# All scores of a segment in one part of the down stage of a retention and SwiGLU kernel

## The chip, the cores and the metric

The kernel runs on one core of a Trainium2 chip. The metric is the device time of one execution in microseconds (us), as the median of several runs. A profiled execution is a run of its own with the hardware profiler on; its time differs a little from that of the runs without it.

Five engines work side by side, each on its own list of instructions in a fixed order: TensorE (PE; its weight loads are shown as PEld), VectorE (DVE), ScalarE (ACT), GpSimd (POOL) and SyncE (SP). SP issues nearly all transfers (DMA) between the chip's memory (DRAM) and the on-chip memory (SBUF). PE writes its results into eight accumulator banks of 128 rows by 512 floats. An engine waits for another by semaphores, and an instruction that waits holds up all that stand behind it on its engine.

## The reference

The kernel computes a retention over 4 batches, 8 heads, 768 positions and 64 dimensions per head, and passes its output through a SwiGLU block:

```python
gamma = 1.0 - 2.0 ** (-5.0 - np.arange(H))          # H = 8
state = zeros(B, H, D, D)                            # B = 4, D = 64
for t in range(S):                                   # S = 768
    state = gamma * state + k[:, :, t]^T v[:, :, t]  # per batch and head
    y[:, :, t] = 1/sqrt(D) * q[:, :, t] @ state
x = y.transpose(0, 2, 1, 3).reshape(B * S, H * D)    # 3072 x 512
g = x @ w_gate                                       # 512 x 1536
out = (g * sigmoid(g) * (x @ w_val)) @ w_out         # 1536 x 512
```

In the kernel the retention is done in chunks of 128 positions. Inside a chunk the scores k q are multiplied by a mask of decays and then applied to v; what came before a chunk enters through a 64x64 state per head, which is decayed and added to from chunk to chunk.

## The kernel before

**Segments and stages.** The 3072 tokens are worked on in four segments, 0 to 3, of 768 tokens each. A segment is three chunk positions of two batches. Each segment has an up stage (the products with w_gate and w_val, 12 tiles f of 128 rows of the hidden dimension) and a down stage (the product with w_out). In segment 0 the up stage uses plain products (lines 896 and 914), and the weights are converted and written back on the way; the up stages of segments 1 to 3 use seven products per tile, called p{f}.0 to p{f}.6 (`up3`, line 1065), each of six 128x384 matmuls. The steps that process these products are called u{f}.0 to u{f}.9; they work in banks 0 and 1, 2+f%2 and 6+f%2.

Numbers are kept in float32 and split into three parts for the matmuls. Helpers record these splits, so many operations share a line: 968 (ACT), 971 (DVE), 974 (POOL or DVE) for weights and hidden values, 977 (ACT), 980 (POOL), 984 (DVE) for the rest. Items live in a ring of slots, and a load into a slot waits until the last reader of the slot is done.

**Down stage.** It consists of 72 steps D{f}.{tok} (`down`, line 1128): for each f in 0 to 11 and each 128-token block tok in 0 to 5, three 128x512 matmuls accumulate into bank tok. A step needs h{f} (the three splits h{f}.0 to .2 of the hidden tile on ACT, DVE and DVE) and the weight item W{f}. In segment 0, W{f} is a load of the plain weights, which d{f}.0 (ACT), d{f}.1 (POOL) and d{f}.2 (DVE) split, and Z{f} writes the result back to DRAM; in later segments W{f} loads the split weights (768 KB). At the end e{tok} brings each bank out.

**Retention within the down stage.** While the down stage of segment s runs, the retention of segment s+1 is computed in steps between the D steps. The chunk positions of the segment are three pairs p = 0, 1, 2, each with a chunk of two batches. For each pair:

- l{n} (`load_pair`, line 752; n = 4p+w with w = 0, 1, 2, 3 for k, q, v and k in its other layout) loads operands to the place that HOME gives; each l{n} moves two tiles of 128x512 floats on SP.
- sc{p} (`scores_of`, line 776): 64 matmuls of 64x64 into two banks.
- dec{p}.0 and .1 (`decayed`, line 786): DVE multiplies each bank with the mask and stores 128x512 into SBUF.
- q{p}.0 and .1 (`scale_q2`, DVE and POOL), k{p}.0 and .1 (`scale_k2`, ACT, in one case POOL) scale q and k.
- A{p}, B{p}, C{p} (`mix_a`, `mix_b`, `mix_c`): matmuls of 64x64 into banks 6 and 7; they give the outputs y and what is added to the state.
- was{p}.z (`decay2`, ACT) decays the state, new{p}.z (`keep_state`) adds to it.
- y{p}.zj (`bring_y`, line 999): 16 copies on ACT per pair out of banks 6 and 7; sum{p}.m and x{p}.n.k make the operands of the next up stage from them.

sc0 uses banks 4 and 5, sc1 and sc2 use banks 6 and 7. The decayed scores of p = 0 and 2 lie in `tmp`, those of p = 1 in `tab` (called `spare`). Since D steps use banks 0 to 5, a D step on bank 4 or 5 that starts the accumulation must wait for dec0, and A, B, C of one pair and sc of the next share banks 6 and 7.

**Order.** The order of all steps is written out by hand: PLAN is a list of 2371 step names, which `run` (line 452) plays, and each step's instructions go to their engines in that order. A name begins with the segment: "0/D0.3" is a step of segment 0's down stage and "1/A0" a step of segment 1's retention. The constants PARTS, COST, LOADS and UNITS and the times given with each step say which steps exist, and matter for the order only where PLAN does not name a step. On PE the three down stages with retention begin like this:

```
segment 0: 1/sc0 D0.0 D0.2 D0.1 D0.4 D0.5 D0.3 1/A0 D1.0 D1.4 1/B0
segment 1: p11.4 2/sc0 p11.6 D0.2 D0.3 D0.4 D0.1 D1.1 D0.5 D0.0 D1.4 D1.5 D1.0 2/A0
segment 2: D0.2 3/sc0 p11.6 D0.1 D0.0 D0.3 D0.4 D1.2 D1.1 D0.5 D1.3 D1.4 D1.5 D1.0 D2.3 3/A0
```

The functions that the diff touches:

Of the kernel before, what the change touches and what calls it, by code (L numbers as in the profile page):

```python
# [18 lines left out]
B, H, S, D = 4, 8, 768, 64  # L19
# [6 lines left out]
L = 3  # L26
# [24 lines left out]
    l0:0 l1:0 A0 A1 s0 U0:0 l0:2 l0:3 a0:1 s1 b0:1 A2 h0 S0:1 m0 K0 x0:2 c0:1 l2:0 x0:1 l2:1  # L51
    l1:3 C0:1 t0 l1:2 V0:0 l3:1 n0:0 s2 a0:0 Q2 l3:0 l2:3 n0:1 b0:0 S0:0 m1 k1 x1:1 x1:2 l2:2
    c0:0 n0:2 U1:1 C0:0 t1 o2 l3:3 g2 s3 n0:3 n0:4 l4:1 p0:0 m2 a1:1 x2:1 k2 q3 b1:1 l4:0 a1:0
    x2:2 S1:1 l5:1 l3:2 n0:5 c1:1 k3 t2 C1:1 o3 b1:0 l5:0 l4:2 g3 v0:0 s4 S1:0 t3 l5:2 c1:0 C1:0
    U2:0 m3 s5 U12:3 U3:1 q5 q4 u0:0 a2 o5 o4 T0:0 n1:0 m4 b2 y0:0 x3:1 x3:2 m5 T0:1 n1:1 n1:3
    T0:2 S2 n1:2 p0:1 v0:1 n1:4 T1:0 x4:1 u0:1 y0:1 a12 n1:5 x5:1 U4:0 T1:1 a3 p1:0 x4:2 u1:0
    p1:1 x5:2 Z0 u1:1 T1:2 c12 v1:0 U5:1 y1:0 v1:1 p0:2 Z1 l5:3 v0:2 c2 C2 b12 y1:1 p1:2 n2:0 a4
    U6:0 u0:2 b3 n2:1 u1:2 v1:2 S12 n2:3 L y0:2 S3 c3 n2:2 U13:2 G2:0 i2:0 n2:4 y1:2 C3 g4 T2:0
    b4 T2:1 n3:0 C12 n2:5 G2:1 i2:1 a5 T2:2 n3:1 Z2 n3:2 S4 n3:3 n3:4 c4 T3:0 C4 W2:0 j2:0 T3:1
    W2:1 G3:1 U7:1 c13 T3:2 G3:0 n4:0 Z12 n3:5 n4:1 i3:1 W3:0 Z3 n4:2 b5 a6 j2:1 i3:0 S5 n4:3  # L60
    G4:1 n4:4 c5 W3:1 T4:0 h2 U8:0 C5 T4:1 T4:2 n4:5 G4:0 a13 i4:1 n5:0 j3:0 n5:1 n5:3 n5:2 b6
    U14:3 i4:0 a7 W4:0 n5:4 j3:1 G5:1 S6 c6 b13 Z4 j4:0 T5:0 T5:1 C6 W4:1 n6:0 U9:1 T5:2 n5:5 b7
    a8 S13 W5:0 G5:0 j4:1 c14 Z5 W5:1 i5:0 i5:1 n6:1 S7 j5:1 n6:3 n6:4 c7 a9 C7 n7:0 n6:2 G6:0
    U10:0 j5:0 b8 G6:1 T6:0 n7:1 n7:3 S8 C13 T6:1 i6:1 i6:0 n6:5 n7:2 c8 Z13 l4:3 a14 n7:4 b14
    W6:1 W6:0 T6:2 C8 T7:0 S14 U15:2 n7:5 n8:0 j6:0 G7:1 j6:1 i7:1 U11:1 C14 b9 G7:0 n8:3 W7:1
    S9 n8:1 c15 n8:2 W7:0 c9 Z6 i7:0 j7:1 a10 P1 C9 n8:4 G8:1 n8:5 T7:1 j7:0 n9:0 b10 Z14 k4
    U16:3 g5 T7:2 S10 T8:0 G8:0 n9:1 a15 b15 P2 c10 Z7 W8:0 T8:1 n9:2 S15 T8:2 Z8 W8:1 C15 C10
    n9:3 i8:1 i8:0 k5 G9:1 Z15 a11 b11 j8:0 j8:1 n10:0 n9:4 S11 n9:5 t4 U17:2 c16 n10:1 G9:0
    T9:0 i9:0 t5 n10:3 n10:2 W9:1 a16 b16 n10:4 n10:5 S16 W9:0 T9:1 j9:0 P0 i9:1 c11 0/h0.0
    G10:0 G10:1 C11 n11:0 j9:1 W10:1 n11:3 i10:0 C16 Z16 i10:1 T9:2 n11:4 Z9 T11:0 T11:1 n11:5  # L70
    a17 b17 T11:2 W10:0 n11:1 T10:0 Z11 0/h0.1 S17 T10:1 j10:0 0/W0 c17 0/h1.0 n11:2 h1 G11:0
    C17 j10:1 i11:0 0/d0.0 G11:1 1/sc0 1/dec0.0 0/W1 1/l3 1/l5 1/q0.0 i11:1 0/h2.0 0/d0.1 0/h0.2
    0/h4.0 0/d1.0 W11:0 0/d0.2 1/k0.0 W11:1 1/l4 j11:0 0/D0.0 0/D0.2 1/dec0.1 0/d1.1 j11:1
    0/h1.1 0/D0.1 0/d1.2 0/W2 1/q0.1 0/D0.4 1/k0.1 1/was0.0 0/D0.5 0/Z0 0/h1.2 0/h2.1 0/D0.3
    T10:2 0/d2.0 Z17 0/h3.0 1/A0 1/new0.0 0/D1.0 0/h3.1 0/Z1 0/d2.1 0/D1.4 1/B0 1/y0.01 0/h4.1
    0/W3 1/y0.05 Z10 1/y0.06 1/y0.03 1/y0.00 1/y0.02 1/y0.04 0/D1.3 0/d2.2 1/begin 1/y0.07
    0/D1.1 1/was0.1 0/h2.2 0/d3.0 0/D1.5 0/h4.2 0/D1.2 1/C0 1/y0.12 1/y0.15 1/y0.11 1/y0.14 0/Z2
    0/d3.1 1/y0.10 0/h3.2 1/y0.17 1/y0.16 0/D2.3 1/y0.13 1/x0.2.0 0/D2.2 1/new0.1 0/d3.2 0/D2.4
    0/W4 1/sum0.0 0/D2.1 1/sum0.1 1/x0.2.1 0/D2.0 0/D2.5 1/x0.1.0 1/l7 0/Z3 0/h5.0 1/sum0.3
    1/x0.1.1 0/d4.0 0/d4.1 1/x0.1.2 1/sc1 1/dec1.1 0/D3.2 1/q1.1 1/sum0.2 1/l6 1/dec1.0 0/D3.4  # L80
    1/q1.0 0/D3.1 0/W5 0/D3.3 0/d4.2 0/h5.1 1/was1.0 1/k1.1 0/D3.5 0/D4.4 1/k1.0 0/D3.0 0/D4.3
    0/h6.0 1/A1 1/l8 0/d5.0 1/x0.2.2 0/D4.2 1/l9 0/D4.5 0/W6 0/d5.1 0/h5.2 0/h6.1 1/x0.0.0
    0/D4.0 0/D4.1 1/new1.0 0/h7.0 0/d6.0 1/B1 1/x0.0.1 0/d5.2 1/y1.01 0/D5.1 0/D5.2 0/Z4 1/y1.06
    1/y1.02 1/y1.00 0/h8.0 0/D5.4 1/y1.05 0/D5.3 0/D5.0 1/y1.07 1/y1.04 0/h6.2 0/W7 1/y1.03
    0/d6.1 1/was1.1 1/x0.0.2 1/C1 0/d7.0 0/h7.1 0/h7.2 1/y1.17 0/Z5 0/d6.2 1/l11 0/D6.2 0/D6.0
    0/D5.5 1/y1.10 1/y1.15 0/h8.1 1/y1.11 1/y1.16 0/d7.1 1/y1.14 1/y1.12 1/y1.13 1/x1.2.0 0/Z6
# [1217 lines left out]
```

## Time and profile before

| what | value |
|---|---|
| median of 3 runs | 648.2 us (647.91 to 648.77) |
| profiled execution | 652.34 us, span 650.5 us, mean granted clock of PE 0.995 |
| PE busy | 635.7 us (98%) |
| PEld busy | 581.5 us (89%) |
| DVE busy | 489.6 us (75%) |
| ACT busy | 392.4 us (60%) |
| POOL busy | 272.3 us (42%) |
| down stage of segment 0, with retention of 1 | 132.5 to 199.7 us |
| down stage of segment 1, with retention of 2 | 286.5 to 354.7 us |
| down stage of segment 2, with retention of 3 | 439.0 to 511.0 us |

Busy times are for the whole span. "Idle before" a group is the time its engine had nothing running just ahead of an instruction of the group, with what ended that time named behind the arrow: another engine, a DMA, or "issue", where nothing that the profile shows was late. A matmul's records show it from its start to a modelled end, so neighbours overlap a little. The granted clock is the share of full speed that the throttle gave PE. The queue named q8 moves instructions, and q1 moves data.

### The profile page before, as it was taken

Reading aid. Unit: us, or ns where it says so; the run is one execution under the profiler, and the core shown is the slowest. Engines: PE = TensorE matmul, PEld = TensorE weight load, DVE = VectorE, ACT = ScalarE, POOL = GpSimd, SP = SyncE. Lnnn points to the kernel's source line nnn. Section 1 sums busy time; section 2 is a strip of 40 time slices with the busy share of each in tenths; the row PEclk is TensorE's granted clock in tenths of the full one; section 3 lists DMA queues with packets and bytes.
Section 4 is the critical chain, followed back from the end, with each engine's and each line's share of the span. In section 5 each row is a group of like instructions: output and inputs, shape, how many; then the busy total and the mean of one; then the engine's idle time right before and its main releaser. Section 6 shows DMA issues by size and latency. Waiting matters only on the chain.

```text
span 650.5 us, 14090 instructions
## 1 busy us (share of the span) xinstructions
PE 635.7 (98%) x5576; PEld 581.5 (89%) x5576; DVE 489.6 (75%) x712; ACT 392.4 (60%) x860; POOL 272.3 (42%) x174
## 2 busy tenths in 40 slices
PE   7999999998999999999999999999899999999997
PEld 6899999986879999997778999998687999999886
DVE  5898688899898887775787769777288876868361
ACT  3688788676855564666766565565576655655211
POOL 0544356533445775820103755640013567662000
PEclk9999999999999999999999999999799999999999
DMA  9999997598858444177765631359378453304564
GB/s 323 374 356 332 350 327 278 198 361 261 300 183 313 152 146 171 36 245 248 247 215 209 235 116 65 123 194 286 115 260 270 156 188 141 133 11 158 177 215 147
DMA packets 50050, 140.13 MB, mean 215 GB/s; under 512 B 4928, under 2 KB 17472, under 8 KB 49984
## 3 DMA queue, kind: packets, MB, share of 16 engines
q1 hardware_dynamic: 49552, 138.57, 61.7%
q8 instruction: 44, 0.72, 0.5%
q10 hardware_dynamic: 432, 0.66, 0.3%
q14 instruction: 22, 0.18, 0.1%
HBM read 109.32 MB, written 29.88 MB: 214 GB/s over the span
## 4 chain that ended last, share of the span: by engine, by line
PE 89%; DMA 4%; DVE 3%; ACT 2%; issue 1%; SPq 0%; ACTq 0%; DVEq 0%
PE bank L1065 40%; PE bank L1128 27%; PE bank L896 13%; PE bank L766 5%; PE bank L914 2%; DMA rawp<-in_w_gate_dram 1%; ACT chunk_x L999 1%; DMA hT<-in_k_n_dram 1%; DMA hT<-in_q_t_dram 1%; DVE oitem L984 0%; DMA loads<-in_v_n_dram 0%; DVE xb L407 0%; PE bank L721 0%; ACT states L865 0%; DVE tmp L407 0%
## 5 line engine op out<-in xcount | busy, mean ns | idle before, releaser
L1128 PE MATMUL bank<-oitem,gitem 128*128 128x512 f32 x864 | 210.9, 398 | 5.6 <-DVE oitem L984 2.9
L1128 PEld LDWEIGHTS bank<-oitem,gitem 128*128 128x128 f32 x864 | 160.5, 189 | 41.8 <-DVE oitem L984 4.4
L974 POOL TENSOR_TENSOR gitem<-gitem 128x768 fp32r<-128x768 f32 x72 | 143.7, 2005 | 100.7 <-DVE gitem L971 74.2
L1065 PE MATMUL bank<-xa,gitem 128*128 128x384 f32 x864 | 160.7, 334 | 0.0
L1065 PEld LDWEIGHTS bank<-xa,gitem 128*128 128x128 f32 x864 | 150.8, 188 | 0.3 <-ACT tmp L1081 0.2
L974 POOL TENSOR_TENSOR oitem<-oitem 128x256 fp32r<-128x256 f32 (+1 forms) x60 | 67.7, 1132 | 70.1 <-DVE oitem L971 56.1
L971 DVE SCALAR_TENSOR_TENSOR gitem<-gitem,loads 128x768 fp32r<-128x768 f32 x72 | 81.1, 1143 | 7.5 <-ACT gitem L968 5.8
L1065 PE MATMUL bank<-xb,gitem 128*128 128x384 f32 x432 | 85.2, 335 | 0.0
L896 PE MATMUL bank<-xa,oitem 128*128 128x384 f32 x480 | 84.2, 335 | 0.0
L896 PEld LDWEIGHTS bank<-xa,oitem 128*128 128x128 f32 x480 | 83.0, 188 | 0.2
L968 ACT ACTIVATE gitem<-loads 128x768 fp32r<-128x768 f32 x72 | 59.2, 842 | 31.8 <-PE bank L1065 24.4
L1065 PEld LDWEIGHTS bank<-xb,gitem 128*128 128x128 f32 x432 | 76.0, 188 | 0.7 <-POOL gitem L974 0.3
L971 DVE SCALAR_TENSOR_TENSOR gitem<-gitem,hT 128x768 fp32r<-128x768 f32 x48 | 50.3, 1053 | 30.1 <-ACT gitem L968 30.0
L968 ACT ACTIVATE gitem<-hT 128x768 fp32r<-128x768 f32 x48 | 40.0, 840 | 41.1 <-PE bank L1128 37.5
L999 ACT COPY chunk_x<-bank 64x128 f32<-64x128 f32 x144 | 35.5, 260 | 33.2 <-PE bank L766 28.4
L793 POOL TENSOR_TENSOR loads<-loads,tab 128x512 f32<-128x512 f32 x9 | 13.7, 1517 | 98.6 <-PE bank L766 83.1
L407 DVE SCALAR_TENSOR_TENSOR gitem<-gitem 128x768 fp32r<-128x768 f32 x48 | 45.9, 962 | 1.1
L1065 PE MATMUL bank<-xb,oitem 128*128 128x384 f32 x216 | 43.6, 336 | 0.0
L1065 PEld LDWEIGHTS bank<-xb,oitem 128*128 128x128 f32 x216 | 37.9, 188 | 0.2
L971 DVE SCALAR_TENSOR_TENSOR oitem<-oitem,loads 128x256 fp32r<-128x256 f32 (+1 forms) x42 | 32.5, 780 | 2.3 <-ACT oitem L968 2.2
L1080 ACT COPY tmp<-bank 128x384 f32<-128x384 f32 x36 | 17.2, 478 | 25.6 <-PE bank L1065 21.4
L980 POOL TENSOR_TENSOR oitem<-oitem 128x512 fp32r<-128x512 f32 x12 | 20.4, 1697 | 27.7 <-ACT oitem L977 27.7
(112 smaller groups left out, 790.0 us busy)
## 6 DMA issues: line engine op xcount, KB each, us to landing
loads<-wup SPq DMA_DIRECT2D x36, 896.0 KB, 4.8
oitem<-wdnt SPq DMA_DIRECT2D x36, 768.0 KB, 4.4
wdnt<-oitem SPq DMA_DIRECT2D x12, 768.0 KB, 4.6
wup<-first SPq DMA_DIRECT2D x9, 896.0 KB, 5.7
rawp<-in_w_gate_dram SPq DMA_DIRECT2D x12, 512.0 KB, 7.2
rawp<-in_w_val_dram SPq DMA_DIRECT2D x12, 512.0 KB, 6.3
rawp<-in_w_out_dram SPq DMA_DIRECT2D x12, 512.0 KB, 6.1
out_dram<-chunk_x SPq DMA_DIRECT2D x22, 256.0 KB, 2.2
```

The costliest lines, as they stand in the source:

```text
L407: stt(o, x, 1.0, y, op0=mul, op1=op)
L766: nc.tensor.matmul(o, a, b, start=start, stop=True, skip_group_check=True)
L793: (pool if i else both)(t, t, qdec, op=mul)
L896: nc.tensor.matmul(o, w[:, a, ts(b, P)], X0[:, a, i, NC - 1 - b], start=a == b == 0, stop=a == 2 and b == NC - 1, skip_group_check=True)
L968: act(o[0], x, AF.Copy, scale=CUT / FAR)
L971: stt(o[1], f32(o[0]), -FAR, x, op0=mul, op1=add)
L974: op(o[2], f32(o[0]), f32(o[1]), op=add)
L980: op(o[1], f32(o[0]), x, op=sub)
L999: copy(cx[half[i], ds(2 * h, 2), c, half[z]], y.rearrange("p (b t) -> p b t", b=2))
L1065: nc.tensor.matmul(o, w[:, a, k], x[:, a, KH - 1 - k], start=start and a == k == 0, stop=a == 2 and k == KH - 1, skip_group_check=True)
L1080: steps = (lambda: copy(p1, x), lambda: tt(c11, z, p1, op=add), lambda: act(gate, c11, AF.Silu, scale=ONE), lambda: copy(u2, x), lambda: c ...
L1128: nc.tensor.matmul(banks[tok], hs[f][:, a, ds(i * TH + u * P, P)], wo[f][:, a], start=f == a == 0, stop=f == NF - 1 and a == 2, skip_group ...
```

## The change

The scores of all three pairs are computed in one step `s` (`all_scores`), 192 matmuls in a row, into banks 2 and 3 (p = 0), 4 and 5 (p = 1) and 6 and 7 (p = 2). The steps sc0, sc1 and sc2 are gone. The six decays follow `s`, and each stores the decayed scores over the k tile that they were made from. HOME gives other places to nearly all operands, some of them in `tab`, `chunk_x` and `tmp`, so that k and q of all pairs can be there at once; several loads are issued earlier (in segment 1: l9, l8 during the up stage, l3, l5, l4 and l2 ahead of W1), and P2, which loaded the first v pair early in segment 0, is now an l2 issued behind W2. was{p}.0 stands with A{p}. PLAN is written anew from segment 0's last up tiles (G7) to the start of segment 3's up stage; 2365 names. The matmuls, the vector operations, the copies and the transfers are the same in number and shape; the waits on semaphores are 244 on DVE (226 before), 263 on ACT (257), 135 on POOL (132), 78 on PE (80) and 172 on SP (176).

On PE the three stages now begin like this:

```
segment 0: D0.0 D0.1 1/s D0.3 D1.3 D0.2 D0.4 D0.5 1/A0 D1.5 D1.1 1/B0
segment 1: p10.6 p11.6 2/s D0.0 D0.4 D0.1 2/A0 D0.5 D0.2 2/B0 D0.3 D1.1
segment 2: p11.6 D0.1 3/s D1.0 D1.1 D0.4 D2.1 D0.5 3/A0
```

The number of D steps between the retention's steps, before and after:

```
segment 0 before: sc0 6 A0 2 B0 4 C0 6 sc1 8 A1 4 B1 5 C1 6 sc2 7 A2 6 B2 5 C2 13
segment 0 after:  2 s 5 A0 2 B0 3 C0 15 A1 3 B1 3 C1 9 A2 9 B2 5 C2 16
segment 1 before: sc0 10 A0 2 B0 5 C0 11 sc1 7 A1 2 B1 4 C1 4 sc2 4 A2 3 B2 6 C2 14
segment 1 after:  s 3 A0 2 B0 12 C0 11 A1 2 B1 6 C1 6 A2 2 B2 6 C2 22
segment 2 before: 1 sc0 12 A0 3 B0 4 C0 10 sc1 6 A1 2 B1 4 C1 6 sc2 6 A2 2 B2 4 C2 12
segment 2 after:  2 s 5 A0 3 B0 2 C0 12 A1 6 B1 5 C1 8 A2 2 B2 5 C2 22
```

The core of the diff, with PLAN cut to the lines around `s` in segment 0:

```diff
@@ PLAN
-    C17 j10:1 i11:0 0/d0.0 G11:1 1/sc0 1/dec0.0 0/W1 1/l3 1/l5 1/q0.0 i11:1 0/h2.0 0/d0.1 0/h0.2
-    0/h4.0 0/d1.0 W11:0 0/d0.2 1/k0.0 W11:1 1/l4 j11:0 0/D0.0 0/D0.2 1/dec0.1 0/d1.1 j11:1
-    0/h1.1 0/D0.1 0/d1.2 0/W2 1/q0.1 0/D0.4 1/k0.1 1/was0.0 0/D0.5 0/Z0 0/h1.2 0/h2.1 0/D0.3
+    0/d1.0 1/l4 C17 0/h1.2 0/d1.1 0/h2.0 T8:2 W11:1 0/d0.2 0/D0.0 j11:0 Z10 0/D0.1 j11:1 T9:2 0/W2
+    1/s 0/h2.1 0/d1.2 1/dec0.1 1/was0.0 0/h3.0 1/l2 1/q0.1 0/D0.3 1/dec0.0 1/dec1.1 0/d2.0 1/dec1.0
+    1/dec2.0 1/k0.0 0/Z0 1/dec2.1 1/q1.1 0/d2.1 0/D1.3 1/q0.0 0/D0.2 0/D0.4 1/q1.0 0/D0.5 1/A0 Z17
...
-    HOME = (2, 3, 4, 0, 1, 2, 3, 4, 0, 1, 4, 0)
+    HOME = (spots[4:6], spots[6:8], spots[2:4], [tmp[:, ts(4, 512)], last],
+            spots[:2], spots[8:], spots[4:6], spots[2:4],
+            [tab[:, ts(i, 512)] for i in range(2)], [chunk_x[:, ts(2 + i, 512)] for i in range(2)],
+            [tmp[:, ts(i, 512)] for i in range(2)], [tmp[:, ts(2, 512)], last])
...
-    spare = tab[:, : 2 * 512]
...
-        w = (0, 1, 2, 3)[w]
-        own = [spots[2 * HOME[n] + i] for i in range(2)] if n < 11 else [tmp[:, ts(2, 512)], last]
-        given.setdefault(p, {})[w] = own
+        given.setdefault(p, {})[w] = own = HOME[n]
...
-    def scores_of(p, own):
-        scored[p] = own = [banks[i] for i in own]
+    def scores_of(p):
...
-                        mm(halves(own[r])[half[c ^ z], z, n], kt[c][half[r], n, half[z]],
+                        mm(halves(banks[2 + 2 * p + r])[half[c ^ z], z, n], kt[c][half[r], n, half[z]],
...
+    def all_scores():
+        for p in range(L):
+            scores_of(p)
+
     def decayed(p, i):
-        att[p, i] = (spare if p % 2 else tmp)[:, ts(i, 512)]
-        o, b = (t.rearrange("p (z n) -> p z n", z=2) for t in (att[p, i], scored[p][i]))
+        att[p, i] = given[p][0][i]
+        o, b = (t.rearrange("p (z n) -> p z n", z=2) for t in (att[p, i], banks[2 + 2 * p + i]))
...
-    for p, b in enumerate((2, 22, 41)):
-        for k, n in enumerate((0, 5, 9, 13)):
-            PARTS[b + n] = "sABC"[k], p
-    COST = {"s": 1.2, "A": 1.4, "B": 1.2, "C": 1.0}
-    LOADS = {5: 7, 6: 15, 7: 19, 8: 19, 9: 27, 10: 39, 11: 43}
-    UNITS = (40, 59, 62)
+    PARTS = {6: ("s", 0)}
+    for p, b in enumerate((12, 27, 44)):
+        for k in range(3):
+            PARTS[b + 4 * k] = "ABC"[k], p
+    COST = {"s": 2.7, "A": 1.4, "B": 1.2, "C": 1.0}
+    LOADS = {6: 20, 7: 24, 10: 10, 11: 24}
+    UNITS = (40, 41, 42)
...
-                    at(t, f"{nxt}/sc{p}", scores_of, p, (R0, R0 + 1) if p else (4, 5))
-                    for i in range(2):
-                        at(d + 0.1 * i, f"{nxt}/dec{p}.{i}", decayed, p, i)
-                        at(d + 0.2 + 0.1 * i, f"{nxt}/q{p}.{i}", scale_q2, p, i)
+                    at(t, f"{nxt}/s", all_scores)
+                    for u in range(L):
+                        for i in range(2):
+                            at(d + 0.2 * u + 0.1 * i, f"{nxt}/dec{u}.{i}", decayed, u, i)
+                            at(d + 0.8 + 3.0 * u + 0.1 * i, f"{nxt}/q{u}.{i}", scale_q2, u, i)
...
+                    if k == 0 and has_old(nxt, p, 0):
+                        at(t - 0.03, f"{nxt}/was{p}.0", decay2, nxt, p, 0)
...
-    for n in range(3, 5):
+    for n in (3, 4, 2, 9, 8, 5):
         at(end + 0.1 + 0.01 * n, f"1/l{n}", load_pair, 1, n)
...
-            for n in range(5):
-                at(t - (18, 13, 12, 5, 4)[n], f"{s + 1}/l{n}", load_pair, s + 1, n)
+            for n, d in {0: 18, 1: 13, 5: 12, 9: 20, 8: 22, 3: 9, 4: 6, 2: 5}.items():
+                at(t - d, f"{s + 1}/l{n}", load_pair, s + 1, n)
```

## The prediction

> **What bounds the kernel now.** I read the page's engine table first, then the chain that ended last, then PE's waits, and then three stretches of the trace: the down stages in which the retention of segments 1, 2 and 3 runs (the change touches nothing after the third). The engine table and the chain:
>
> ```profile
> PE 635.7 (98%) x5576; PEld 581.5 (89%) x5576; DVE 489.6 (75%) x712; ACT 392.4 (60%) x860; POOL 272.3 (42%) x174
> PE 89%; DMA 4%; DVE 3%; ACT 2%; issue 1%; SPq 0%; ACTq 0%; DVEq 0%
> ```
>
> PE sets the end. Counts of PE's instructions do not change, so only its idle time and its clock can move the result. The three stages (start:end in us, length, busy time of PE, PEld, DVE, ACT, POOL, granted clock, DMA share, GB/s):
>
> ```profile
> core 0: us, PE busy (x) PEld busy (x) DVE busy (x) ACT busy (x) POOL busy (x), PEclk, DMA share, GB/s
> 132.50:199.70 67.20, 64.31 (x890) 50.31 (x889) 62.28 (x83) 46.28 (x133) 26.50 (x15) 1.00 0.83 289
> 286.50:354.70 68.20, 67.90 (x972) 54.93 (x972) 50.75 (x79) 45.85 (x136) 9.70 (x6) 1.00 0.70 244
> 439.00:511.00 72.00, 69.30 (x966) 55.37 (x965) 51.17 (x77) 45.10 (x134) 11.26 (x7) 0.95 0.69 226
> ```
>
> PE idles 2.89, 0.30 and 2.70 us there. Only the first stage has a second engine near its limit: DVE, 62.28 of 67.20. PE's waits in these stages (us in total, times, longest), and the instructions that waited:
>
> ```profile
> PE bank L1128 <- DVE oitem L984: 2.9, 2, 1.7
> PE bank L1128 <- issue: 2.7, 1, 2.7
> PE bank L766 <- ACT chunk_x L999: 0.3, 1, 0.3
> ```
>
> ```profile
> 156.22 0.96 PE L1128 MATMUL bank<-oitem,gitem 128*128 128x512 f32 x3 [1.69 <-DVE oitem L984]
> 185.18 0.49 PE L1128 MATMUL bank<-oitem,gitem 128*128 128x512 f32 x1 [1.20 <-DVE oitem L984]
> 439.64 1.16 PE L766 MATMUL bank<-loads 64*64 64x64 f32 x64
> 458.31 3.15 PE L1128 MATMUL bank<-oitem,gitem 128*128 128x512 f32 x7 [2.70 <-issue]
> ```
>
> The 2.70 us are "issue": no engine was late. What ended it is a transfer of PE's instructions. The first two lines are from the page's queues and from the DMA view of 455.6 to 457 us, the others are windows like those above:
>
> ```profile
> q8 instruction: 44, 0.72, 0.5%
> q8 instruction: 1, 0.02, 4.9%
> 455.60:458.30 2.70, 0.01 (x1) 0.00 (x0) 0.00 (x0) 2.63 (x10) 0.00 (x0) 0.85 0.09 27
> 457.50:464.30 6.80, 5.99 (x59) 4.44 (x58) 0.00 (x0) 0.87 (x3) 0.00 (x0) 0.50 0.01 4
> ```
>
> q8 moves 44 packets of 16 KB. PE has 11235 instructions (5576 loads, 5576 matmuls, 83 of semaphores), so a packet holds 256. Laid against PE's instructions, packet n starts only after instruction 160+256n was issued, by a delay that differs; a transfer takes about 1.0 us. Packet 31 started at 455.75, 5.38 us after its trigger (instruction 8096), and ended at 456.86. PE ran dry at instruction 8385, 289 after the trigger, and went on at 458.31, 1.45 us after the end. So the 289 instructions behind a trigger must last for the delay and 2.45 us more. Then the clock: it stood at 0.50 from 457.48 for 6.83 us, which cost half, 3.4 us. The waits of 1.69 and 1.20 left it at 1.00. The event at 455.6 thus cost 2.70 + 3.4 = 6.1 us.
>
> **The change, part by part.** Times are summed against the profiled execution: span 650.5, 652.34 in all, 1.84 around the span; the runs' median 648.2 lies 4.1 below it. A difference under 0.2% (1.3 us) can't be told from none.
>
> *Same work.* The scores are three groups of 64 small matmuls before and after (1.09 to 1.16 us each, about 17 ns per matmul); six decays of 0.69 on DVE, the scalings, A, B, C, copies and splits keep count and shape. DVE has 18 more waits and ACT 6 more, POOL 3 fewer, PE 2 fewer. No row has the time of a wait that is already met; taken at 0, bounded above by about 1 us, since DVE has 4.9 us idle in the first stage and 17 in the others. Scores written over k_t cost nothing: only the scores read k_t, and the next load into these places comes a segment later.
>
> *First stage (segment 0).* The scores went first, then D0.0; now D0.0 and D0.1 go first, so d0.2 (DVE) is wanted 1.09 earlier, at 131.9. These two rows show how such a split lasts when POOL runs beside it, and a decay:
>
> ```profile
> 131.22 1.78 DVE L984 SCALAR_TENSOR_TENSOR oitem<-oitem 128x512 fp32r<-128x512 f32 x1
> 133.50 0.69 DVE L789 TENSOR_TENSOR tmp<-bank,local 128x512 f32<-128x512 f32 x1
> 130.90 1.56 POOL L980 TENSOR_TENSOR oitem<-oitem 128x512 fp32r<-128x512 f32 x1 [1.01 <-ACT oitem L977]
> ```
>
> d0.2 comes at 131.8 to 133.0: a wait of 0 to 1.1. After s, D0.3 wants bank 3, so PE waits for a decay that stands on DVE behind products, T9:2, h2.1 and d1.2: 0.3 to 2. Together 0 to 3; I take 1.3, nearest to the two waits that DVE causes now. Against this, d4.2 and d9.2, whose lateness is the 1.69 and 1.20, are wanted 1.77 and 1.21 us later, because one group of scores is no longer in the middle; DVE's idle gaps in the stage (1.21 waiting for the scores, 2.34 for the copies of y, 1.86) mostly fill. Both waits go: -2.9. Late next is d1.2 or the decay in front of A0. Sum -1.6, bounds -2.9 and +1.5. l2 (moved on SP behind W2) lands near 138, A0 comes at 139.5: hidden; l4 near 133 for a need at 133.9; if that cover goes, up to 1 us.
>
> *Second stage.* The 0.30 goes, as p=2's scores no longer wait for banks that the copies of y empty. l3, l5, l4 and l2 now stand on SP ahead of W1; W1 still waits for p10.6 and has until D1.1, 9 us after s. Nothing here waits for new data: -0.3.
>
> *Instruction transfers.* Score matmuls pass at 17 ns, so 192 in a row use up PE's queue. In segment 1, s is instructions 4931 to 5319, and 5024 is a trigger: the 289 behind it last 2.55 us. That is 0.1 more than is needed with no delay at all. The smallest delay after a trigger in these stages is 0.80, so a wait is likely; with a mean delay of the stage it is 2.43. The delays seen: stage one 3.06, 4.98, 3.11, 1.68, 1.25, 1.17; two 2.27, 1.40, 3.07, 2.54, 2.98, 4.41, 1.07; three 3.49, 5.38, 4.99, 3.69, 3.69, 0.84, 0.80, 2.81. For each packet I take the mean, over its stage's delays, of what exceeds the time it has. Tested on the kernel now, whose tight packets have 5.04 (31), 5.21 (36), 6.24, 6.35, 6.35, this gives 2.45 us in all; 2.70 were measured. In the new order: packet 8 has 5.76 us, 9 has 5.32, 11 has 5.99 (0.28, 0.42, 0.24); 19 has 2.55 (2.43); 20, 22, 24 have 5.84, 6.01, 4.62 (0.15, 0.12, 0.63); 30, 31, 32 have 5.44, 5.72, 5.63 (0.79, 0.61, 0.67). Sum 6.3 in place of 2.7: +3.6. Bounds: with the smallest delay everywhere only packet 19 waits, 0.7; with each stage's largest everywhere, 20.
>
> *Clock.* The old event's 3.4 goes with its wait, since s moves the triggers of the third stage. Does the new one bring it back? Rows: 1.69 did not halve the clock, 2.70 did; 2.43 is nearer to 2.70, and 192 small matmuls stand ahead of it where full ones stood. I take +3.4, bounds 0 and 6.8 (a second wait in stage three).
>
> [...]
>
> *Sum.* 652.34 - 1.6 - 0.3 + 3.6 - 3.4 + 3.4 = 654.0, and 4.1 less, as the runs stood to the profile before: **649.9**.
>
> **The rivals.**
>
> - *The clock stays.* Same waits, none long enough: 649.9 - 3.4 = **646.5**. For it: 1.69 and 1.20 left the clock at 1.00. Against: 2.70 did not. It decides where the threshold between 1.69 and 2.70 lies. [...]
> - *The transfers are hidden, and it is faster.* If the 4.1 us between profile and runs are mostly the event at 455.6, delays are shorter without a profile; 2.0 of the 6.1 are then left in the runs before. With the smallest delay (0.80) the new order waits 0.7 once: 648.2 - 1.9 - 2.0 + 0.7 = **645.0**. Against: four pairs are now issued close together just ahead of s, and each moves half a megabyte in front of the packet.
> - *DVE is late in the first stage.* After s, D0.3 and A0 stand behind decays which stand behind a split for d. If the decay for bank 3 ends over 2 us after s, the start costs 3 and the waits at d4.2 and d9.2 stay, as DVE (62.28 of 67.20) makes up nothing: +1.5 to +2 instead of -1.6, **653.3**. For it: DVE is nearly full. Against: its gaps of 1.21, 2.34 and 1.86 are waits for scores and copies, which the new order fills. In stage three W2, released by p11.6, lands 4.7 to 8 us after s for a need at 6.0: up to 2 us of the same sign.
>
> **How the numbers follow.** Transfers late and the clock halved: 0.42, 649.9, own range 647.5 to 652.5. Clock stays: 0.20, 646.5 (645 to 648). Hidden: 0.16, 645.0 (643.5 to 646.5). DVE late: 0.22, 653.3 (651 to 655). Faster is under 646.9, slower over 649.5. Of the first case 0.30 is slower and 0.12 same; of the second 0.14 faster and 0.06 same; the third is faster, the fourth slower. Faster 0.30, same 0.18, slower 0.52. Leaving out the lower third of the third case and the upper half of the fourth gives 644.6 to 654.0.
>
> **What would show it.** A wait called issue in segment 1's s, ended by an instruction packet, 2 to 3 us long, and the clock at 0.50 behind it. The wait at D3.4 of segment 1 gone. In the first stage no wait of D4 and D9 on DVE, but one of 0.3 to 2 on the decays behind s. In stage two no wait for y's copies. The forecast is wrong if s runs through without a gap, if the gap leaves the clock at 1.00, or if a wait on DVE over 2 us stands at D0.3 or A0 of the first stage.

## The result, and the profile after

The changed kernel takes 670.2 us (median of five runs, 669.3 to 672.9, the profiled execution being the slowest of them), against 648.2 before: a ratio of 1.0343, 95% interval 1.0323 to 1.0363. That is 22 us slower and far outside the forecast range. Below, "over the kernel before" is a ratio less one, times 648.2; for the changed kernel it is 22.2, give or take 1.3.

One sentence of the description of the change is wrong, and it matters: PLAN does not differ from G7 on only. The first 160 steps (the retention of segment 0 and the first plain products) stand in another order too, from the second step on; the 150 or so after them are as before.

The page of the changed kernel, engines, chain and granted clock:

```profile
PE 641.8 (96%) x5576; PEld 586.9 (88%) x5576; DVE 505.2 (75%) x712; ACT 390.4 (58%) x860; POOL 262.1 (39%) x174
PE 76%; DVE 7%; DMA 6%; ACT 5%; issue 4%; POOL 1%; SPq 1%; DVEq 0%; ACTq 0%; POOLq 0%
PEclk8799999989998999997999999999999999999999
```

PE has fallen from 98% to 96% of a longer span, the chain runs through DVE, DMA, ACT and "issue" where it ran through PE, and the clock line dips in the first slices and at three later places where it dipped once. PE's waits (us in total, times, longest), and those of the down stages with the instruction that waited:

```profile
PE bank L757 <- issue: 6.3, 3, 4.3
PE bank L1120 <- DVE oitem L976: 5.1, 2, 3.2
PE bank L627 <- DMA hT<-in_k_t_dram: 2.7, 2, 2.4
PE bank L627 <- DVE xa L398: 2.5, 1, 2.5
PE bank L683 <- POOL hT L648: 2.4, 1, 2.4
PE bank L757 <- ACT chunk_x L991: 2.1, 4, 0.8
PE bank L1120 <- issue: 1.1, 1, 1.1
```

```profile
141.36 2.07 PE L1120 MATMUL bank<-oitem,gitem 128*128 128x512 f32 x4 [3.25 <-DVE oitem L976]
208.09 2.12 PE L1120 MATMUL bank<-oitem,gitem 128*128 128x512 f32 x7 [1.82 <-DVE oitem L976]
309.89 0.48 PE L757 MATMUL bank<-chunk_x,tab 64*64 64x64 f32 x4 [4.26 <-issue]
```

The waits at L627 and L683 lie in the first 23 us, in the steps I had not seen move. The first line of the second fence is D0.0 of segment 0, the second the end of that stage, the third the last of the 192 score matmuls of s in segment 1. Windows of the first 32 us and of segment 0's down stage, before (start:end, length, busy time of each engine, granted clock, DMA share, GB/s):

```profile
core 0: us, PE busy (x) PEld busy (x) DVE busy (x) ACT busy (x) POOL busy (x), PEclk, DMA share, GB/s
0.00:32.00 32.00, 26.80 (x361) 24.07 (x362) 21.81 (x38) 16.79 (x33) 9.59 (x12) 1.00 0.99 348
131.40:199.50 68.10, 65.21 (x896) 51.25 (x895) 63.18 (x83) 47.38 (x138) 27.60 (x16) 1.00 0.83 289
```

and after, with the first 33 us and the same down stage; the last two rows are the scores of s in segment 1 and the wait at their end:

```profile
0.00:33.00 33.00, 24.26 (x279) 21.86 (x280) 17.47 (x30) 15.18 (x33) 9.66 (x12) 0.84 0.95 335
137.50:214.30 76.80, 69.52 (x959) 54.65 (x958) 63.71 (x87) 49.23 (x138) 25.86 (x18) 0.96 0.79 285
302.40:305.60 3.20, 3.20 (x189) 3.00 (x189) 2.98 (x6) 3.20 (x13) 1.82 (x2) 1.00 1.06 262
305.60:309.90 4.30, 0.04 (x3) 0.01 (x2) 0.45 (x1) 1.39 (x6) 0.68 (x1) 0.84 0.96 338
```

PE does less in the first 33 us at a clock of 0.84. The first down stage is 8.7 us longer although DVE is no busier in it: DVE idles 13 us where it idled 5. At s in segment 1 the DMA engines are at a share of 1.06, and the packet of instructions that PE needs starts only 4.23 us after its trigger.

Profile against profile, from the starts of D0.0 and of the last D step in each segment: the first steps cost 6.0 us (first D at 137.48 in place of 132.53, and the 1.1 of scores that stood ahead of it now comes later), segment 0's down stage 8.7, the steps from there to the end of segment 1's down stage 7.4; segment 2 wins 3.05, and 0.9 is lost at the end: 20.0. The 3.05 are won against a profile of before that has the event at 455.6; what the runs say of segment 2 comes further down.

### The profile page after: what moved, and what is told of

It is laid out like the page before. It is cut to its first block, busy times and chain, and to the rows that moved or that the text cites. A ratio compares the mean times of both kernels' runs of the same rounds, so it can differ in the third digit from the quotient of the medians.

```text
span 670.7 us, 14111 instructions
## 1 busy us (share of the span) xinstructions
PE 641.8 (96%) x5576; PEld 586.9 (88%) x5576; DVE 505.2 (75%) x712; ACT 390.4 (58%) x860; POOL 262.1 (39%) x174
## 4 chain that ended last, share of the span: by engine, by line
PE 76%; DVE 7%; DMA 6%; ACT 5%; issue 4%; POOL 1%; SPq 1%; DVEq 0%; ACTq 0%; POOLq 0%
PE bank L1057 37%; PE bank L1120 22%; PE bank L888 7%; PE bank L757 5%; DMA wdnt<-oitem 4%; PE bank L906 3%; ACT chunk_x L991 1%; DVE first L398 1%; DMA hT<-in_k_n_dram 1%; DMA hT<-in_v_n_dram 1%; DVE gitem L963 1%; DVE tmp L398 1%; DVE oitem L963 1%; ACT states L857 1%; PE bank L698 1%
## 5 line engine op out<-in xcount | busy, mean ns | idle before, releaser
L966 POOL TENSOR_TENSOR gitem<-gitem 128x768 fp32r<-128x768 f32 x72 | 138.3, 1927 | 143.6 <-DVE gitem L963 126.1
L963 DVE SCALAR_TENSOR_TENSOR gitem<-gitem,loads 128x768 fp32r<-128x768 f32 x72 | 85.7, 1198 | 5.1 <-ACT gitem L960 4.9
L972 POOL TENSOR_TENSOR oitem<-oitem 128x512 fp32r<-128x512 f32 x12 | 17.9, 1495 | 44.3 <-ACT oitem L969 34.5
L963 DVE SCALAR_TENSOR_TENSOR oitem<-oitem,loads 128x256 fp32r<-128x256 f32 (+1 forms) x42 | 34.4, 823 | 0.0
L1075 DVE TENSOR_TENSOR hT<-bank,tmp 128x384 f32<-128x384 f32 x36 | 19.9, 554 | 15.5 <-PE bank L1057 12.8
L1074 DVE TENSOR_TENSOR hT<-bank,tmp 128x384 f32<-128x384 f32 x36 | 20.0, 555 | 14.5 <-PE bank L1057 11.0
```

The costliest lines, as they stand in the source:

```text
L963: stt(o[1], f32(o[0]), -FAR, x, op0=mul, op1=add)
L966: op(o[2], f32(o[0]), f32(o[1]), op=add)
L1074: lambda: copy(p5, wb), lambda: tt(h1, x, p5, op=add),
L1075: lambda: tt(h0, wb, u2, op=add), lambda: tt(h0, h0, gate, op=mul),
```

## The experiments

Unless said otherwise, an edit is to the changed kernel. In the diffs PLAN is shown by the steps that move.

### The first steps, the instruction packets, and one step of DVE

**First steps as before.**

```diff
-PLAN: l0:0 A0 U0:0 l1:0 a0:1 A1 s0 s1 l0:2 A2 ...
+PLAN: l0:0 l1:0 A0 A1 s0 U0:0 l0:2 l0:3 a0:1 ...    (first 160 steps of before)
```

> The changed kernel with the first 160 steps of PLAN in the order of the kernel before (the retention of segment 0 and the first plain products); all else as changed. Theory: the changed order of these first steps costs 6.0 us (first D step at 137.5 instead of 132.5, with 1.1 of scores now behind it), so 664.2 here, and the waits of 2.35, 2.40 and 2.53 us in the first 21 us are gone. Rival: what is lost there is made up later, because DVE and the loads are behind anyway in segment 0's down stage: 668 or more.

664.6 us, ratio 1.0257 (1.0241 to 1.0273), 16.7 over the kernel before. The first steps cost 5.5, give or take 1.6, as the theory said, and nothing is made up later. In the changed order the load U0:0 of raw weights (SP) stands ahead of l1:0; PE then waits 2.35 us at 8.3 for the k that l1:0 brings.

**Triggers of the packets moved.**

```diff
+    def spin(n): n times a 64x64 matmul of the warm-up data
-PLAN: ... 0/d0.2 0/D0.0
+PLAN: ... 0/d0.2 0/spin 0/D0.0        (n = 100)
```

> The changed kernel with 100 extra matmuls of 64x64 (17 ns each) ahead of D0.0 of segment 0, where PE waits 3.25 us for DVE anyway. They do no work of the reference; they only move where in PE's instructions the packets are asked for: 200 instructions earlier in the program. Theory (instruction transfer): the trigger inside segment 1's s now lies where the 289 instructions behind it last over 5.9 us, so the issue wait of 4.26 us and the halved clock behind it (6.83 us at half speed, 3.4 us) are gone: 670.2 - 7.7 = 662.5; by the same count one packet near the start of segment 2's s is tighter (3.7 us), which may give back up to 2. Rival (the wait is one for data or banks that the profile can't name): the wait stays at its place with 3 to 4.5 us and the time is 670 to 672.

681.9 us, 34.2 over the kernel before. The size of the block was wrong: its 100 fp32 matmuls stand in the trace as 200 pairs of load and matmul, and in a single quadrant of the array these took 59 ns each, so the block took 11.87 us and moved the triggers by 400 instructions, not 200. Less the block it is 670.1, as slow as the changed kernel, although D0's wait of 3.25 is now hidden behind the block. But the wait moved as a packet must move it; PE in s of segment 1 and of segment 2:

```profile
313.71 0.39 PE L761 MATMUL bank<-loads 64*64 64x64 f32 x11 [1.34 <-issue]
474.24 0.69 PE L761 MATMUL bank<-chunk_x,tab 64*64 64x64 f32 x10 [4.46 <-issue]
```

The 4.26 us at the end of s in segment 1 are gone (a wait of 1.34 is in another place of s), and s of segment 2, which now holds trigger 8352 in its first half, waits 4.46. Two more waits on issue came: 1.49 in s of segment 0 and 1.67 in A0 of segment 1. No data and no bank had changed.

**The same on the kernel before.**

```diff
     warm_up(8)
+    spin(44)
```

> The kernel before with 44 extra matmuls of 64x64 behind the warm-up at the start, where PE then waits for loads: 88 instructions more ahead of all triggers. By the count no packet has then less than 6.6 us. Theory: the issue wait of 2.70 us and its 3.4 us of halved clock are gone; in the runs without profile 2.0 to 6.1 us of them are left to win: 642 to 646.2. Rival (the event is of the profiled execution alone): 648.2 as before, within 0.7.

654.5 us (1.0105, 1.0082 to 1.0128). Again 5.9 us of matmuls, and they were not hidden: the first D step starts 5.05 later. The wait of 2.70 us is gone, and all four down stages ran at full clock (the mean of the profile is 0.997); one wait of 1.28 on issue came in its place. The runs are 6.8 over; take the 5.05 off, and they have gained nothing from it, which the shorter warm-up below asks again without the block.

**One step of DVE moved.**

```diff
-PLAN: 0/h0.2 T8:1 0/d0.1 ... 0/h1.2 0/d1.1 0/h2.0 T8:2 W11:1 0/d0.2 0/D0.0
+PLAN: 0/h0.2 0/d0.1 0/d0.2 T8:1 ... 0/h1.2 0/d1.1 0/h2.0 T8:2 W11:1 0/D0.0
```

> The changed kernel with one vector step, d0.2 of segment 0, moved ahead of T8:1, h1.2 and T8:2 on DVE; nothing else. Theory: the wait of 3.25 us of the first D step goes (d0.2 then ends near 136.4, the step is at 137.7) and with it the 3.41 us of halved clock behind it (1.7 us): 4.9 us at the place, of which DVE, now later with T8:1 and T8:2, gives back at most 2: 665 to 668. Rival (DVE is the bound of this stage, so any order of it costs the same): 669.5 to 670.5.

671.4 us, 23.4 over the kernel before: no gain. The wait at D0 fell from 3.25 to 0.64, and 1.88 us of wait for j11 (DVE) came at s, which needs banks 2 and 3 empty; the clock was halved all the same (mean of the profile 0.984, 0.982 as changed). The rival was right about this move: it was worth nothing.

### More of segment 0, and packets once more

**Two blocks, of a better size** (with the first steps as before). The matmuls of the first block go round four quadrants of the array, those of the second round two.

```diff
     warm_up(8)
+    spin(50, 2, 3)
-PLAN: ... 2/p0.0
+PLAN: ... 2/spin 2/p0.0               (n = 20)
```

> The changed kernel with the first 160 steps of the kernel before, and with two blocks of extra 64x64 matmuls that do no work of the reference: 50 behind the warm-up at the start and 20 ahead of p0.0 of segment 2. They move the triggers of the instruction packets by 200 instructions up to there and by 280 behind; by the count no packet then has less than 5.4 us, where segment 1's s had 2.7. Theory (instruction transfer): no issue wait over 1 us in any s, no halved clock at segment 1's s; 664.6 (the same without the blocks) - 7.0, and 2 to 3 for the blocks: 659.6 to 660.6. Rival (the wait belongs to s, whatever the packets): it stays, 666 to 668.

665.1 us, 16.5 over: no gain, though the wait at s of segments 1 and 2 is gone as counted. The blocks take some 3 us of it (the first D step starts 1.74 later than without them, the second block lasts 1.4). The wait came back where the triggers now lie:

```profile
143.29 1.50 PE L761 MATMUL bank<-chunk_x,tab 64*64 64x64 f32 x55 [1.97 <-issue]
307.21 0.58 PE L761 MATMUL bank<-loads 64*64 64x64 f32 x18 [1.81 <-issue]
```

The first is in s of segment 0, where the packet came 8.07 us after its trigger, the second in A0 of segment 1. With 192 small matmuls in a row, and A and B close behind them, 256 instructions passed too fast somewhere in each of the three positions of the triggers that were tried (as changed, moved by 400, and here).

**Loads of the next up stage behind W11** (first steps as before).

```diff
-PLAN: 1/B2 0/W10 1/L2 0/d10.0 ... 0/Z8 0/D8.1 1/L1 ... 0/D9.5 0/W11
+PLAN: 1/B2 0/W10 0/d10.0 ... 0/Z8 0/D8.1 ... 0/D9.5 0/W11 1/L2 1/L1
```

> The changed kernel with the first 160 steps of the kernel before, and with the loads L2 and L1 of the next up stage issued behind W11 of segment 0 instead of ahead of it. Theory: W11 waits for its slot until Z8 has landed, and Z8 stands on SP behind L2, L1; with them later, W11 lands earlier, the wait of 1.82 us for d11.2 and the 1.7 us of halved clock behind it go: 664.6 - 3.5 = 661.1. Rival: L1 and L2 are then late for the splits of the up stage, and the same 3.5 us are lost at p1 and p2: 664 to 666.

662.7 us, 14.8 over, 1.9 less than without (give or take 1.6); the wait of 1.82 and its halved clock are gone (mean clock of the profile 0.992, 0.990 without the move). SP's queue in the changed kernel shows why it was there:

```profile
190.97 0.42 SPq L1029 DMA_DIRECT2D loads<-wup  x1
191.44 0.42 SPq L1115 DMA_DIRECT2D wdnt<-oitem  x1
191.91 0.43 SPq L1029 DMA_DIRECT2D loads<-wup  x1
200.54 0.32 SPq L1102 DMA_DIRECT2D oitem<-wdn  x1
```

L2, Z8, L1 and W11. W11 needs the slot that Z8 writes back, and Z8, between two loads of 896 KB, took 9.0 us to land; with the loads behind it W11 was issued 5.1 us after Z8. Half of the gain was lost again, to a wait of 1.3 us for the operands x.

**Three sums of DVE behind the decays** (first steps as before).

```diff
-PLAN: ... T8:1 0/d0.1 ... T8:2 W11:1 0/d0.2 0/D0.0 j11:0 ... T9:2 0/W2 1/s ... 1/dec2.1
+PLAN: ... 0/d0.1 0/d0.2 ... W11:1 0/D0.0 j11:0 ... 0/W2 1/s ... 1/dec2.1 T8:1 T8:2 T9:2
```

> The changed kernel with the first 160 steps of the kernel before, and with DVE's T8:1, T8:2 and T9:2 (sums of the up weights, 4 to 5 us at this place) moved behind the six decays, d0.2 directly behind d0.1. Theory (order: s needs bank 2 and 3, so j11 and d0.2 stand on the path, and the sums do not have to be ahead of them): the wait of 2.80 us at D0 goes, with 1.7 us of halved clock, 664.6 - 4.5 = 660.1. Rival (amount: DVE is full, so what is moved is waited for at the next step, h2 or d1.2 or the decays): 663.5 to 665.5, with a wait of 2 to 4 us at another step of D0 to D2.

664.3 us, 16.7 over: nothing. The wait at D0 fell to 0.21, but 2.62 us came at D3 and 0.90 ahead of it: W3 had been issued behind the write-backs Z9 and Z8, which follow these sums. My theory fell, for this place.

**A shorter warm-up in the kernel before.**

```diff
-    warm_up(8)
+    warm_up(5)
```

> The kernel before with 5 matmuls of warm-up instead of 8, 12 PE instructions fewer ahead of all triggers; by the count no packet has then less than 6.2 us, where packet 31 had 5.04. Theory: no issue wait in segment 2's down stage and no halved window behind it; in runs without a profile, whose mean clock was 0.996 to 1.000, that is worth 0.5 to 2.5 us: 645.2 to 647.2. Rival: the runs without a profile do not have the wait: 647.7 within 0.6; or the shorter warm-up costs at the start, 648 to 650.

647.9 us; ratio 0.9993 (0.9983 to 1.0004), no difference that can be told. Yet the profiled execution fell from 652.34 to 647.20; the longest of PE's waits in its down stages are now those on DVE, and no wait on issue is left:

```profile
PE bank L1128 <- DVE oitem L984: 2.1, 2, 1.7
```

The first D step starts at 132.30 (132.53 before), so a loss at the start that would hide a gain is not to be seen. Segment 2, from the last D step of segment 1 to its own, is 4.8 us shorter, in this profile as in the one with the block. So the event, 4.8 us rather than the 6.1 of the prediction, was one of the profiled execution; of the runs without a profile the interval leaves it at most 1.1 us.

### The change, segment by segment

For these the code keeps both ways, and PLAN goes from one order to the other at p2.0 of a segment.

```diff
+    OLD = {...}                         (segments whose retention is as before)
-        given.setdefault(p, {})[w] = own = HOME[n]
+        given.setdefault(p, {})[w] = own = (WAS if s in OLD else HOME)[n]
+    def score_banks(s, p):
+        return ((4, 5), (6, 7), (6, 7))[p] if s in OLD else (2 + 2 * p, 3 + 2 * p)
```

> The kernel before in which only segment 0 (its first steps, its down stage and the retention of segment 1 in it) is as changed; from p2.0 of segment 1 on all is as before. Theory (by stages: 6.0 for the first steps, 8.7 for the first down stage): 648.2 + 14.7 = 662.9. Rival (the slow start is a cost of the loads that the changed order issues ahead for later stages, and does not come without them): 655 or less.

> The kernel before in which only the retention of segment 2, in the down stage of segment 1, is as changed (all scores in one part). Theory: the issue wait of 4.26 us at the end of s and the halved clock behind it (3.4): 648.2 + 7.4 = 655.6. Rival (what is lost there is owed to the state in which the changed segment 0 hands over, not to s): 648 to 650.

> The kernel before in which only the retention of segment 3, in the down stage of segment 2, is as changed. Profiled execution against profiled execution the stage won 3.05 us, of which 6.1 were the event at 455.6 and 3 were lost again. Theory (the event costs the runs without a profile only about 1, as the kernel with a shorter warm-up showed): 648.2 - 1 + 3 = 650.2, with issue waits in or behind s. Rival (the gain is there without a profile too): 645.2.

> The changed kernel in which segment 0 is as before: the sum of the two others with only a later segment changed. Theory (the losses of the stages add up): 670.2 - 14.7 = 655.5, up to 2 more where the profile hides the gain of segment 2. Rival (they don't add up, because one late stage gives the next time to catch up): 650 or 660.

| as changed | median us | ratio (95% interval) | over the kernel before |
|---|---|---|---|
| segment 0 alone | 662.5 | 1.0207 (1.0188 to 1.0226) | 13.4 |
| retention of segment 2 alone | 654.7 | 1.0094 (1.0075 to 1.0113) | 6.1 |
| retention of segment 3 alone | 651.1 | 1.0044 (1.0027 to 1.0060) | 2.9 |
| both of these | 657.4 | 1.0137 (1.0119 to 1.0155) | 8.9 |
| all | 670.2 | 1.0343 (1.0323 to 1.0363) | 22.2 |

13.4 + 6.1 + 2.9 = 22.4: the losses add up, within 2 us. With the retention of segment 2 alone there is one new wait of any size, and the clock falls to half behind it; PE around the end of s:

```profile
289.81 0.92 PE L764 MATMUL bank<-chunk_x,tab 64*64 64x64 f32 x45
295.35 0.33 PE L764 MATMUL bank<-chunk_x,tab 64*64 64x64 f32 x4 [4.62 <-issue]
```

With the retention of segment 3 alone there is a shorter wait in the middle of s, and one of 0.79 for copies of y:

```profile
445.26 0.27 PE L763 MATMUL bank<-loads 64*64 64x64 f32 x2 [1.61 <-issue]
```

Segment 2, counted as above, takes 153.4 us there, against 151.6 in the two profiles of the kernel before that lack the event: s loses in this segment too.

### What is left in segment 0

**Left-over work back ahead of the down stage.** All steps up to W0 as before (T8, T9, Z8, Z9 among them), the loads l3, l5, l8, l9 put between them.

> The changed kernel in which all steps of segment 0 up to W0 stand as in the kernel before, so that T8:1, T8:2 and T9:2 (DVE) and the write-backs Z8 and Z9 of the up weights come ahead of the down stage again; the down stage itself, with s, stays as changed. Theory (the change pushed this left-over work of the up stage into the start of the down stage, where it delays d0.2 on DVE and W3 in the transfers): the wait of 2.8 us at D0 and its halved clock (1.7) go, and none of 2 us or more comes at D1 to D3: 664.6 - 4.5 = 660.1. Rival (s itself, with its six decays and j11 ahead of it, is what makes DVE late): 663.5 to 665.5, a wait of 2 to 3 us at D0, s or D2.

> The same with L2 and L1 behind W11. Theory (both repairs of segment 0 add up, as different waits: 4.5 and the 2.0 that the second gave alone): 658.1. What is then left over the kernel before is s in segments 1 and 2 (7.9 together) and at most 2 in segment 0. Rival (one limit stands behind the other, so that the second gives nothing): as the run without it.

669.9 and 666.5 us (1.0334 and 1.0287). Both had the load l8 into tab ahead of the copy h1 of the mask out of tab, so their retention used a wrong mask, at the same amount of work; ACT waited 5.94 us for that load and D0 with it. They answer nothing on the question. Again, with the copy first:

```diff
-PLAN: T10:1 j10:0 1/l8 1/l9 h1 1/k0.1 T10:2 n11:2 0/W0 c17 0/h1.0 G11:0
+PLAN: T10:1 j10:0 0/W0 c17 0/h1.0 n11:2 h1 1/l8 1/l9 1/k0.1 T10:2 G11:0
```

> As the run before it with the left-over work of the up stage ahead of the down stage, but with the copy h1 of the mask (ACT, out of tab) ahead of the load l8, which takes its place in tab; in the other order ACT had waited 5.94 us for that load, and D0 with it, so that run did not answer the question. Theory (sums and write-backs of the up weights behind the start of the down stage make d0.2 and W3 late): no wait over 1 us at D0, 660.1. Rival (s itself, with j11 and six decays ahead of the next steps, is what makes DVE late): a wait of 2 to 3 us at D0, s or D2 stays, 663.5 to 665.5.

> The same with L2 and L1 behind W11. Theory (the repairs add up): 2.0 less than the run without it, 658.1. Rival: as the run without it.

663.3 us (1.0230, 1.0199 to 1.0260) and 659.5 us (1.0173, 1.0140 to 1.0205). The first is 1.8 less than without, give or take 2.2: not shown, and the wait at D0 is still 2.33. The second, with W11's repair as well, is 5.5 less (give or take 2.3): no less than the 1.8 and 1.9 of the two alone, so nothing speaks against their adding up. DVE and POOL of the first, ahead of that wait:

```profile
126.31 0.41 DVE L402 SCALAR_TENSOR_TENSOR first<-first 128x256 f32<-128x256 f32 x1
128.78 5.13 DVE L402 SCALAR_TENSOR_TENSOR gitem<-gitem 128x768 fp32r<-128x768 f32 x2
133.84 0.68 DVE L980 SCALAR_TENSOR_TENSOR oitem<-oitem 128x512 fp32r<-128x512 f32 x1
```

```profile
128.03 1.97 POOL L976 TENSOR_TENSOR oitem<-oitem 128x512 fp32r<-128x512 f32 x1 [3.66 <-ACT oitem L973]
129.97 3.13 POOL L558 TENSOR_TENSOR first<-first,rawp 128x1024 int32<-128x1024 int32 x1
```

Two splits of DVE take 5.13 us beside two operations of POOL; the same two take 1.82 in the next run. The second POOL operation is C17.

```diff
-PLAN: G11:0 0/d0.0 ... 0/d1.0 1/l4 C17 0/h1.2
+PLAN: G11:0 C17 0/d0.0 ... 0/d1.0 1/l4 0/h1.2
```

> The kernel of the last run (sums and write-backs ahead of the down stage, L2 and L1 behind W11) with one more step moved: C17, a POOL operation of 3.1 us on the last up weights, from between d1.0 and h1.2 to ahead of d0.0, where the kernel before has it. Theory (DVE's splits h0.2 and h1.2 took 5.1 us together instead of 1.9 because C17 and d0.1, d1.1 ran on POOL beside them): the two take under 3 us, the wait of 2.2 us at D0 falls under 0.5: 659.5 - 2 = 657.5. Rival (DVE has too much to do at this place whatever runs beside it): 659 to 660, with the wait at D0 or s.

> The kernel before, with segment 0 (and the retention of segment 1 in it) as in the run above: all scores in one part there, with the repairs; from p2.0 of segment 1 on as before. Theory (in segment 0 s itself costs little, what cost there were the steps around it; in segments 1 and 2 s costs 7.9 together): 657.5 - 7.9 = 649.6, or 0.5 to 1.5 over the kernel before. Rival (s costs in segment 0 as well, through instruction packets or DVE): 652 or more.

659.3 us (1.0152, 1.0117 to 1.0188): the splits take 1.82 as expected, but a sum takes 2.19 and d0.2 1.75 beside POOL instead, and the wait at D0 is 2.07. No gain can be told. With segment 0 so repaired and all else as before, 652.2 us (1.0051, 1.0031 to 1.0072), 3.3 over the kernel before. PE's waits there of over 1 us in total, from the first D step on:

```profile
PE bank L1129 <- DVE oitem L985: 2.1, 1, 2.1
PE bank L1066 <- DVE xa L402: 1.3, 1, 1.3
PE bank L763 <- ACT chunk_x L1000: 1.2, 4, 0.5
PE bank L1066 <- DVE chunk_x L1149: 1.1, 1, 1.1
```

So of the 13.4 us of segment 0 some 10 (give or take 2) were owed to steps other than s that the new order had moved: 5.5 to the first steps, the rest to W11 and the left-over work. 3.3 (give or take 1.3) remain. In this profile stand the wait of d0.2 at D0 with a halved clock window behind it, the copies of y (0.94 of the 1.2 in segment 0), and two waits in the up stage that follows, 1.32 for x, which came with W11's repair, and 1.10; the waits at D4 and D9 are gone against this. That s itself causes the 3.3 is not shown: the wait at D0 is ahead of it. In the run before, with the same segment 0, DVE is busy without a gap from 121.7 to 136.8. Which of its steps would have to go was not tried, and no version beat the kernel before.

## Why the prediction was wrong, point by point

**The instruction packets: right in place and kind, too small.** A wait at the end of s in segment 1 was forecast at 2.43 us with the clock halved for another 3.4. It was 4.26 us, and 3.4 to 4.6 in the other profiles with s and the triggers at this place, with 6.83 us at half clock, of which 1.34 still lay in the wait, so 2.7 lost. (The prediction read 3.4 from the event in the same way; there 0.83 of the 6.83 lay in the wait, so 3.0.) The mis-sized term is the delay: I took the mean over a stage, 2.53, and it was 4.23, and 3.4 to 5.3 in the others. Four load pairs were issued just ahead of it, and the DMA engines stood at a share of 1.06; that these loads made it long is likely from the delays listed at the end, but no run moved them. Over the whole kernel the mean gave 6.3 us of such waits; 7.4 were measured.

**The event at 455.6: a gain that the runs did not have.** In the sum, "+ 3.6 - 3.4 + 3.4" with a constant 4.1 taken off carried the whole 6.1 us of that event into a sum for the runs. The 4.1 was no constant: the changed kernel's profiled execution is only 2.7 over the median, and that with the shorter warm-up 0.7 under it. The rival of hidden transfers held the clue (most of the 4.1 us between profile and runs being this event), and I gave it 0.16. The shorter warm-up took the event out of the profile and left the runs where they were (0.9993). The third stage, segment 2's, was forecast to win 4.0 and lost 2.9.

**Segment 0: the step that failed.** The sum had -1.6 for this stage, with bounds -2.9 and +1.5; it lost about 8 (13.4 less the 5.5 of the first steps). "Together 0 to 3; I take 1.3" was for d0.2 (0 to 1.1) and the decays behind s (0.3 to 2). Measured were 3.25 for d0.2 alone, at D0.0, and nothing at the decays: I took d0.2 to keep its time on DVE, but the new order put the sums T8:1 and T8:2 ahead of it, and these took 2.65 and 1.48 us beside POOL. "Both waits go" held for d4.2 and d9.2, but what was late next was not on my list: W11, behind Z8, behind L2 and L1, whose places (UNITS, PLAN) I read and did not price: 1.82. Each of these two halved the clock for a window of 3.41 us, 1.7 us each, and I had counted a halved clock only behind 2.4 us and more. Three waits for copies of y (0.18, 0.49 and 0.67) were not in the sum either.

**The first steps: not in the sum at all.** I compared PLAN by the set of steps done at a point further on, found it the same, and took the order for the same. That left out 5.5 us. The prediction took PE's idle time from the three down stages alone, and asked nothing of the first 30 us, where PE had 5 us of idle time and the DMA engines were at a share of 1.0.

**The rival "DVE is late in the first stage" (0.22, 653.3)** had the direction of segment 0, but not the place: it put the wait behind s, at D0.3 or A0, where none came, and kept the waits at D4 and D9, which went. It had no clock and no W11, and it came on top of a gain.

**Right were:** PE stays the bound and its counts do not change; l2 and l4 are hidden; no wait in the second stage for the banks of p=2; no wait on W2 in the third.

## What to carry to other kernels

Work that is taken together to save something else can cost by what it does to the instruction stream: here a row of 192 matmuls of 17 ns ran dry of instructions (4.26 us in s of segment 1), and where it stood against the packets decided, with data and banks unchanged. When an order is rewritten, compare it as an order, from the first step, and price each queue that a moved load passes, the loads of the next stage too. A wait of up to 1.69 us cost only itself here; one that halved the clock cost up to half a window more (1.7 of 3.41 us) for each window that then ran at half rate, so forecast waits and clock together.

## What the runs showed of the hardware

- **Instructions of PE.** In the twenty profiles PE never came to the instruction 289 behind a trigger sooner than 1.2 us after the end of that packet on q8; in 56 cases it came there 1.2 to 1.65 us after, as behind packet 31 of the kernel before (1.45). The delay between trigger and packet went from nothing to 8.07 us. It went with the data on the DMA engines: where their share in the 1 us behind the trigger was under 0.2, the delay was 1.0 us in the mean (216 packets), where it was 0.8 and more, 3.1 (495 packets).
- **The clock.** It fell in windows of 3.413 us (in the changed kernel it stood at 0.50 from 141.30 to 144.71, from 209.56 to 212.98 and, two windows, from 308.55 to 315.38), on a grid that lies differently in each profile (an edge at 4.76 us there, at 6.92 in the kernel before). Of the windows that ran at full clock, from 20 us on and in all twenty profiles, the next ran at half clock behind each of the 27 in which PE idled for 2.0 us and more, and behind 8 of the 11 with 1.81 to 1.97 (1.82 above; 1.97 and 1.81 with the two blocks). It did so behind none of the 23 with 1.2 to 1.69, and a wait of 1.82 that fell half into each of two windows (the sums behind the decays) did nothing. So my estimate from these counts is that about half a window of idle time, 1.7 to 2.0 us, decided, not the length of the wait alone. The three of 1.88 to 1.91 that left the clock alone stay open; two of them are the start of the long waits at s, as here with the retention of segment 2 alone, where PE is busy for 1.50 and 0.70 us and only the third window is halved:

```profile
289.23:292.64 3.41, 1.50 (x98) 1.36 (x90) 1.79 (x3) 2.95 (x13) 2.24 (x2) 1.00 1.00 359
292.64:296.05 3.41, 0.70 (x6) 0.59 (x6) 0.40 (x1) 0.00 (x0) 0.00 (x0) 1.00 0.73 218
296.05:299.47 3.42, 3.42 (x13) 2.21 (x15) 2.15 (x4) 0.00 (x0) 0.00 (x0) 0.50 0.03 8
```

  The changed kernel's runs had mean clocks of 0.979 to 0.987, the kernel before 0.993 to 1.000.
- **DVE beside POOL.** A sum of 128x256 took 0.41 us alone; of the 24 in the first 150 us of the changed kernel eight took 0.87 to 2.65, each beside a POOL operation. Products of 128x384 read out of banks took 0.55 in both kernels. The 25 sums into `first` between 32 us and the first D step (of 128x256, and of 128x512 with 0.68 us alone) took 12.7 us before and 20.2 after; POOL was at work beside them for 4.0 us of it before and 10.7 after:

```profile
134.90 0.96 DVE L398 SCALAR_TENSOR_TENSOR gitem<-gitem 128x768 fp32r<-128x768 f32 x1
135.77 2.65 DVE L398 SCALAR_TENSOR_TENSOR first<-first 128x256 f32<-128x256 f32 x1
139.22 1.48 DVE L398 SCALAR_TENSOR_TENSOR first<-first 128x256 f32<-128x256 f32 x1
```

  The last two are T8:1 and T8:2, ahead of d0.2 in the changed kernel; POOL was busy with C17 from 135.07 for 3.08 us. T8:1, 2.65 us in place of 0.41, ended 0.27 us after C17, and T8:2, 1.48 us, 0.28 after the split that POOL ran from 138.96 for 1.46. What in the chip made DVE wait no trace shows.
- **Small matmuls.** 64x64 matmuls passed at 17 ns each in the scores at full clock, which go round the four quadrants of the array (189 in the 3.20 us of s above), at 35 ns in the second of the two blocks, which used two (40 in 1.4 us), and at 59 ns in the block that used one (200 in 11.87 us). The first of the two blocks, at the start of the kernel, used four and passed at 28 ns (100 in 2.77 us), so the number of quadrants is not all of it.
